# Column-tiled pooling scores for three blocks, loads of a batch spread out, the 2-chunk unit last

## The chip, the cores and the metric

The kernel runs on one core of a Trainium2 chip. A core has five engines that run at the same time and wait for one another through semaphores: TensorE (PE in the profile; its weight loads are shown apart as PEld), VectorE (DVE), ScalarE (ACT), GpSimd (POOL) and SyncE (SP). Data move between main memory and the on-chip memory by DMA; GpSimd and SyncE issue the DMAs here. Matmuls write to PSUM, [...], and DVE or ACT take the results out.

The metric is the device time of one launch in microseconds. The kernel before took 338.13 us (median of 5 runs, 337.91 to 340.12).

## The reference

Two operators follow one another. The first pools a batch's 12,544 tokens into 32 rows by attention from 32 fixed rows (the inducing points), and then lets each token attend to these 32 rows. The second is a feed-forward layer with the larger of two projections.

```python
B, N, m, C = (4, 12544, 32, 128)          # x: (B, N, C), inducing: (m, C)
def mab(q, kv):
    s = scale * (q @ kv.transpose(0, 2, 1))
    a = exp(s - s.max(-1)) ; a /= a.sum(-1) + 1e-09
    return a @ kv
h = mab(I, x)                             # 32 pooled rows per batch
y = mab(x, h)                             # (B * N, C) tokens
out = maximum(y @ w1, y @ w2) @ w_out     # d_ff = 1024
```

The types are float32 in and out.

## The kernel before

The 12,544 tokens of a batch lie as 128 partitions by 98 chunks. A chunk is one column of 128 tokens. Blocks of 16 chunks are called p1 blocks; there are six of them and one of 2 chunks. Inside, x is kept in half precision, once as loaded (`xn`, ten rotating tiles) and once transposed (`xT`, two tiles, one for odd batches and one for even ones).

**Pooling.** For every block, the scores of 128 tokens against the 32 inducing rows are a matmul with the transposed x as weights (`u_scores`, L226, for batch 0; `p1_scores`, L324, for the others). ScalarE takes the exponential into a tile `et` (L235, L333). A matmul with `xn` as weights and `et` as moving data adds up the pooled rows `h` (L260, L346). The sums of the exponentials come from a matmul with a column of ones in batch 0 (L251), and from additions on GpSimd into `eacc` in the other batches (L363, L366). There, `small_fold` (L373) folds the 16 chunks of `eacc` to one in four additions on GpSimd, and `small_h` multiplies it with ones on TensorE (L380) and scales `h`. `small_hwd` (L440) and `small_m1` (L460) then prepare the weights of the second part for that batch.

**Batch 0** comes first and has nothing to hide behind. Its blocks are cut into units; the last blocks are cut finer, and `units` is reordered so that the unit of 2 chunks comes before the last three units (L83). All loads of the units are issued by GpSimd in the order of `units` (L179, L125), the first block by SyncE. The loop at L718 and the lines after it (L726 to L742) write out the order of TensorE's work: transposes of unit i on TensorE (`u_transpose`, L210, copied out by DVE and ACT at L215 and L218), scores of unit i-1, accumulation of unit i-2. After the last unit come the loads of batch 1 (L743), `u_h` with eight more transposes (L271), `u_hwd` (L408), and the first staged blocks.

**The main part** is a sequence of 196 bursts (L803). A burst writes four PSUM banks with the projections of up to 512 columns (L564); DVE (L595) or ACT (L599) take them out with a maximum against zero, and one output tile of an earlier burst is finished with 16 matmuls (L626), a DVE multiplication (L652) and, every second one, a store (L662). The stores of batches 0 to 2 are issued by GpSimd, the others by SyncE. Batch 0 has bursts 0 to 48, batch 1 has 49 to 97, batch 2 has 98 to 146 and batch 3 has 147 to 195.

Between the bursts, `jobs` hold the pooling of the next batch, put there by `at(g, ...)` (L772 to L787). A job runs after the burst with its number, in program order. For the batch after batch b, with `first[b]` the first burst of b: the transposes by DMA (`transpose_batch`, seven DMAs on SyncE, behind a one-element copy on GpSimd at L135 that waits for the last load), the scores and the accumulation of each block, the loads of the batch after that (`load_x`, L120, seven DMAs on GpSimd, one every two bursts, behind the one-element copy of L143), and then the four small steps: fold, h, hwd and m1. For batch 1 they come after bursts 40, 43, 44 and 45, for batches 2 and 3 after 40, 42, 43 and 44 of the batch that runs.

**What sets the order.** Every engine works through its own instructions in program order. The program order is written out by hand as described; which of DVE and ACT takes a bank out, and which bank is used, is decided while the program is built, by a small model of engine times (`Model`). GpSimd's order is that of the calls: stores, loads, additions, folds and the one-element copies stand in one line. Each DMA that GpSimd issues uses one of eight semaphores in turn.

Of the kernel before, what the change touches and what calls it, by code (L numbers as in the profile page):

```python
# [9 lines left out]
F16 = mybir.dt.float16  # L10
F32 = mybir.dt.float32
AF = mybir.ActivationFunctionType
# [39 lines left out]
def kernel(  # L52
# [9 lines left out]
    nc = tc.nc  # L62
    B, N, C = x.shape
    M = inducing.shape[0]
# [4 lines left out]
    scale = 1.0 / math.sqrt(C)  # L69
    HS = 2.0**-14  # L70
    P1B = 16
# [3 lines left out]
    units = []  # L75
    for i, (_, n) in enumerate(p1_blocks):
# [3 lines left out]
            units += [(i, 0, n // 2), (i, n // 2, n // 2)]  # L80
        else:
            units.append((i, 0, n))
    units = units[:-4] + units[-1:] + units[-4:-1]  # L83
    NU = len(units)
    last = NU - 4

    consts = ctx.enter_context(tc.tile_pool(name="consts", bufs=1))
    big = ctx.enter_context(tc.tile_pool(name="big", bufs=1))
    etp = ctx.enter_context(tc.tile_pool(name="etp", bufs=7))
    e2p = ctx.enter_context(tc.tile_pool(name="e2p", bufs=5))  # L90
    smp = ctx.enter_context(tc.tile_pool(name="smp", bufs=2))
    relup = ctx.enter_context(tc.tile_pool(name="relup", bufs=3))
# [7 lines left out]
    model = Model()  # L100
    uid = [0]

    def bank(shape, dtype=F32):
        i = model.bank()
        uid[0] += 1
        return i, psum.tile(shape, dtype, name=f"ps{uid[0]}", tag=f"bank{i}", bufs=1)
# [6 lines left out]
    xT_tiles = [big.tile([128, K, 128], F16, name=f"xT{i}", tag=f"xT{i}") for i in range(2)]  # L113

    def xn_of(b, i):
        return xn_tiles[(NP1 * b + i) % NXN]
# [47 lines left out]
    inducingT = consts.tile([C, M], F16, name="inducingT")  # L164

    with tc.manual_schedule(engines={ET.PE, ET.DVE, ET.Activation, ET.Pool, ET.SP}):
# [28 lines left out]

        st = [dict() for _ in range(B)]


        pool0 = {}

        def u_transpose(i):
            t, g0, n = units[i]
            xn = xn_of(0, t)
            step = 8
            for g in range(g0, g0 + n, step):
                m = min(step, g0 + n - g)
                bi, ps = bank([128, 8, 128], F16)
                end = 0.0
                for j in range(m):
                    nc.tensor.transpose(ps[:, j, :], xn[:, g + j, :], identity16)  # L210
                    end = model.pe(0.056)
                k = p1_blocks[t][0] + g
                dst = xT_tiles[0][:, k : k + m, :]
                if i >= last - 2 or (g // step) % 2 == 0:
                    nc.vector.tensor_copy(out=dst, in_=ps[:, 0:m, :])  # L215
                    model.bank_free[bi] = model.ev("DVE", 64 * m, end)
                else:
                    nc.scalar.copy(out=dst, in_=ps[:, 0:m, :])  # L218
                    model.bank_free[bi] = model.ev("ACT", 128 * m, end)

        def u_scores(i):
            t, g, n = units[i]
            k = p1_blocks[t][0] + g
            bi, ps = bank([128, P1B * M])
            for j in range(n):
                nc.tensor.matmul(  # L226
                    out=ps[:, j * M : (j + 1) * M],
                    lhsT=xT_tiles[0][:, k + j, :],
                    rhs=inducingT,
                    start=True,  # L230
                    stop=True,
                )
                end = model.pe(0.025, model.bank_free[bi])
            et = etp.tile([128, P1B, M], F16, name=f"et_0_{i}", tag="et")
            nc.scalar.activation(  # L235
                out=et[:, 0:n, :], in_=ps[:, 0 : n * M], func=AF.Exp, scale=scale
            )
            model.bank_free[bi] = model.ev("ACT", n * M, end)
            pool0["et", i] = et

        def u_accum(i):
            t, g, n = units[i]
            et = pool0.pop(("et", i))
            xn = xn_of(0, t)
            if i == 0:
                for name in ("h", "sum"):
                    pool0[name] = bank([128, 512])
                    model.bank_free[pool0[name][0]] = 1e9
            for j in range(0, n, 4):
                w = min(4, n - j) * M  # L250
                nc.tensor.matmul(  # L251
                    out=pool0["sum"][1][0:w, 0:1],
                    lhsT=et[:, j : j + w // M, :],
                    rhs=ones16,
                    start=(i == 0 and j == 0),
                    stop=(i == NU - 1 and j + 4 >= n),
                )
                model.pe(0.025)
            for j in range(n):
                nc.tensor.matmul(  # L260
                    out=pool0["h"][1][:, 0:M],
                    lhsT=xn[:, g + j, :],
                    rhs=et[:, j, :],
                    start=(i == 0 and j == 0),
                    stop=(i == NU - 1 and j == n - 1),
                )
                model.pe(0.025)
# [422 lines left out]
        bi, ps = bank([128, 512])  # L690
# [6 lines left out]
        for q in range(4):  # L697
            r = slice(32 * q, 32 * (q + 1))
            nc.vector.tensor_copy(
                out=same_m[r, :, :], in_=identity32[r, None, r].broadcast_to((32, 4, M))  # L700
# [17 lines left out]
        for i in range(last - 1):  # L718
            u_transpose(i)
            if i >= 1:  # L720
                u_scores(i - 1)
            if i >= 2:
                u_accum(i - 2)
            if i < last - 2:
                keep_warm(1)
        u_transpose(last - 1)  # L726
        u_scores(last - 2)
        u_accum(last - 3)
        u_transpose(last)
        u_scores(last - 1)  # L730
        u_transpose(last + 1)
        u_accum(last - 2)
        u_transpose(last + 2)
        u_scores(last)
        u_accum(last - 1)
        u_transpose(last + 3)
        u_scores(last + 1)
        u_scores(last + 2)
        u_accum(last)
        u_scores(last + 3)  # L740
# [14 lines left out]
        for b in range(B):  # L755
            blks = [blk for blk in flat if blk.b == b]
            lead_in = 3 if b == 0 else 0
            for i, blk in enumerate(blks):
                j = i if i < lead_in else i - (i - lead_in) % 2
# [9 lines left out]
        def at(g, f, *a):  # L769
            jobs.setdefault(g, []).append((f, *a))  # L770

        for b in range(B - 1):  # L772
            nb, g = b + 1, first[b]

            t0, l0 = (9, 24) if b == 0 else (-3, 16)
            at(g + t0, transpose_batch, nb)
            if nb + 1 < B:
                at(g + l0, hold_loads, nb)
            for i in range(NP1):
                s = g + (14 + 4 * i if b == 0 else 5 + 5 * i)  # L780
                at(s, p1_scores, nb, i)
                at(s + 2, p1_accum, nb, i)
                if nb + 1 < B:
                    at(g + l0 + 2 * i, load_x, nb + 1, i)
            d = 1 if b == 0 else 0
            for s, f in ((40, small_fold), (42, small_h), (43, small_hwd), (44, small_m1)):
                at(g + s + (0 if f is small_fold else d), f, nb)  # L787


        def load_wf():  # L790
# [64 lines left out]
```

The softmax here doesn't subtract the row's maximum and nothing guards it: scores larger than these inputs give would overflow.

## Time and profile before

| | before |
|---|---|
| time, median of 5 | 338.13 us |
| time of the profiled execution | 338.73 us |
| its span, from the first to the last instruction | 337.0 us |
| TensorE busy | 329.0 us (98%) |
| weight loads busy | 263.1 us (78%) |
| DVE busy | 297.0 us (88%) |
| ScalarE busy | 271.5 us (81%) |
| GpSimd busy | 94.6 us (28%) |
| granted TensorE clock | 0.999 |

The page sums one execution. Its busy times count an engine's own instructions, and its chain follows the end of the program back to what released each step. A line of groups or of the timeline names the source line, the engine, what is written and read with its shape, and at the end the idle time before it with what ended that idle time. In the timeline the first two numbers are the start and the length in us, and xN means that N instructions in a row were merged. The matmuls' ends are modelled, so the starts are the better numbers for them.

### The profile page before, as it was taken

To read this page: it belongs to the slowest core of one execution; us is meant where nothing else is said; L and a number is where in the kernel's file an instruction comes from. 1 tells how busy PE (TensorE), PEld (TensorE's weight loads), DVE (VectorE), ACT (ScalarE), POOL (GpSimd) and SP (SyncE) were. 2 spreads that over 40 slices of the span, in tenths; PEclk is the share of its full clock that TensorE was granted. 3 is DMA by queue.
4 is the path that set the end of the run, shared out by engine and by line. 5 is a ranking of instruction groups with operands and counts; after the bars stand their busy time and mean duration, and the time that the engine had idled before them with its cause. 6 is when DMAs were issued, how large, how long until landed. Compare 5 with 4: busy or idle time off the path is not lost.

```text
span 337.0 us, 14526 instructions
## 1 busy us (share of the span) xinstructions
PE 329.0 (98%) x6352; PEld 263.1 (78%) x6352; DVE 297.0 (88%) x628; ACT 271.5 (81%) x523; POOL 94.6 (28%) x166
## 2 busy tenths in 40 slices
PE   8999999999999999999999999999999999999995
PEld 3776787888878878888877878888777777878875
DVE  1459999999989999999998999999998998999993
ACT  4749978777898887887898877787899989888881
POOL 6242113176741234542341232332252100000000
PEclk9999999999999999999999999999999999999999
DMA  8999899999919986994219992221221222222222
GB/s 213 208 207 215 195 194 196 218 257 234 265 74 227 223 189 161 191 247 136 95 67 189 241 211 79 97 95 64 96 97 65 111 95 75 94 90 95 96 97 109
DMA packets 54143, 51.47 MB, mean 153 GB/s; under 512 B 41536, under 2 KB 42464, under 8 KB 54080
## 3 DMA queue, kind: packets, MB, share of 16 engines
q0 software_dynamic: 11552, 32.38, 38.1%
q1 hardware_dynamic: 42528, 18.17, 25.8%
q8 instruction: 49, 0.80, 1.0%
q14 instruction: 14, 0.11, 0.1%
HBM read 28.33 MB, written 25.69 MB: 160 GB/s over the span
## 4 chain that ended last, share of the span: by engine, by line
PE 91%; DMA 4%; ACT 2%; DVE 1%; POOL 1%; issue 1%; POOLq 0%
PE ps L626 57%; PE ps L564 19%; PE ps L579 4%; DMA xn<-in_x_dram 4%; PE ps L324 2%; PE ps L346 2%; PE ps L499 2%; ACT relu L599 2%; DVE o L652 1%; POOL xn L125 1%; PE ps L520 1%; DVE relu L595 1%; PE ps L210 1%; PE ps L260 0%; PE ps L440 0%
## 5 line engine op out<-in xcount | busy, mean ns | idle before, releaser
L599 ACT ACTIVATE relu<-ps 128x512 f16<-128x512 f32 x445 | 235.9, 601 | 41.6 <-PE ps L564 29.7
L595 DVE TENSOR_SCALAR relu<-ps 128x512 f16<-128x512 f32 x339 | 218.0, 679 | 5.0 <-PE ps L564 3.9
L626 PE MATMUL ps<-woutp,relu 128*128 128x128 f16 x3136 | 208.7, 220 | 0.0
L626 PEld LDWEIGHTS <-relu 128*128 128x128 f16 x3136 | 175.6, 98 | 31.3 <-issue 21.6
L652 DVE TENSOR_TENSOR o<-ps,rp 128x256 f32<-128x256 f32 x196 | 81.7, 417 | 16.3 <-PE ps L626 11.6
L662 POOL DMA_DIRECT2D out_dram<-o x75 | 41.3, 551 | 149.7 <-DVE o L652 102.2
L564 PE MATMUL ps<-e,hwd 32*128 32x256 f16 (+1 forms) x1632 | 82.3, 268 | 0.7 <-ACT relu L599 0.2
L564 PEld LDWEIGHTS <-hwd 32*128 32x128 f16 x1632 | 26.9, 92 | 19.0 <-issue 3.5
L579 PE MATMUL ps<-m,e 32*128 32x128 f16 x372 | 29.8, 214 | 0.8
L579 PEld LDWEIGHTS <-e 32*128 32x128 f16 x372 | 18.3, 92 | 7.1 <-issue 4.2
L366 POOL TENSOR_TENSOR eacc<-eacc,et 128x512 f32<-128x512 f32 (+1 forms) x18 | 18.5, 1030 | 0.3
L333 ACT ACTIVATE et<-ps 128x512 f16<-128x512 f32 (+1 forms) x21 | 11.4, 545 | 5.1 <-PE ps L324 5.1
L120 POOL DMA_DIRECT2D xn<-in_x_dram x21 | 11.4, 545 | 4.4 <-DMA xn<-in_x_dram 1.8
L215 DVE COPY xT<-ps 128x1024 f16<-128x1024 f16 (+2 forms) x10 | 5.8, 596 | 5.9 <-PE ps L210 5.8
L509 ACT ACTIVATE e<-ps 128x512 f16<-128x512 f32 (+1 forms) x21 | 10.9, 578 | 0.0
L324 PE MATMUL ps<-inducingT,xT 128*128 128x32 f16 x294 | 10.6, 176 | 0.3 <-ACT relu L599 0.3
L346 PE MATMUL ps<-et,xn 128*128 128x32 f16 x294 | 10.6, 176 | 0.0
L324 PEld LDWEIGHTS <-xT 128*128 128x128 f16 x294 | 9.5, 96 | 0.4 <-issue 0.4
L346 PEld LDWEIGHTS <-xn 128*128 128x128 f16 x294 | 9.5, 96 | 0.0
L499 PE MATMUL ps<-xT,hT 128*32 128x512 f16 (+2 forms) x120 | 8.7, 350 | 0.0
L191 PE MATMUL ps<-warm 128*128 128x512 f16 x22 | 7.5, 484 | 1.2 <-DVE warm L167 1.2
L210 PE MATMUL ps<-identity,xn 128*128 128x128 f16 x98 | 7.3, 219 | 0.9 <-DMA xn<-in_x_dram 0.5
(79 smaller groups left out, 120.8 us busy)
## 6 DMA issues: line engine op xcount, KB each, us to landing
out_dram<-o POOLq DMA_DIRECT2D x72, 256.0 KB, 3.7
xn<-in_x_dram POOLq DMA_DIRECT2D x21, 512.0 KB, 8.9
out_dram<-o SPq DMA_DIRECT2D x24, 256.0 KB, 2.0
xf<-in_x_dram SPq DMA_DIRECT2D x2, 512.0 KB, 4.1
wf<-in_moe_w_dram SPq DMA_DIRECT2D x2, 512.0 KB, 5.4
xn<-in_x_dram POOLq DMA_DIRECT2D x3, 256.0 KB, 12.2
out_dram<-o POOLq DMA_DIRECT2D x3, 128.0 KB, 5.1
xT<-xn SPq DMA_TRANSPOSE x21, 7.2
```

The costliest lines, as they stand in the source:

```text
L120: nc.gpsimd.dma_start(out=xn_of(b, i)[:, 0:n, :], in_=xr[b, :, k0 : k0 + n, :])
L324: nc.tensor.matmul(out=ps[:, j * M : (j + 1) * M], lhsT=xT_tiles[b % 2][:, k0 + j, :], rhs=inducingT, start=True, stop=True,)
L346: nc.tensor.matmul(out=ps[:, 0:M], lhsT=xn[:, j, :], rhs=et[:, j, :], start=(j == 0), stop=(j == n - 1),)
L366: nc.gpsimd.tensor_add(out=acc, in0=acc, in1=et[:, 0:n, :])
L499: nc.tensor.matmul(out=ps[32 * q : 32 * (q + 1), 0 : self.width], lhsT=st[self.b]["hT4"][:, 32 * q : 32 * (q + 1)], rhs=xT[:, q % self.g], ...
L564: nc.tensor.matmul(out=ps[:, jj * w : (jj + 1) * w], lhsT=st[blk.b]["hwd"][r, 128 * jb : 128 * (jb + 1)], rhs=blk.e2[r, 128 * self.t0 : 12 ...
L579: nc.tensor.matmul(out=part.fin[q][1][:, 128 * s : 128 * (s + 1)], lhsT=part.blk.e2[r, 128 * tt : 128 * (tt + 1)], rhs=st[part.blk.b]["m1" ...
L595: nc.vector.tensor_scalar(out=dst, in0=src, scalar1=0.0, scalar2=None, op0=ALU.max)
L599: nc.scalar.activation(out=dst, in_=src, func=AF.Relu)
L626: nc.tensor.matmul(out=o, lhsT=self.relu[:, jb, q, tt, :], rhs=woutp[:, jb, :], start=(start and s == 0 and jb == 0), stop=(not start and ...
L652: nc.vector.tensor_mul(self.osb[:, h : h + 2, :], ps[:, 0:256].rearrange("p (s c) -> p s c", s=2), rp.broadcast_to((128, 2, 128)),)
L662: eng.dma_start(out=outr[blk.b, :, k : k + nst, :], in_=self.osb[:, 0:nst, :])
```

## The change

Five edits are made together.

- `units` is no longer reordered: the unit of 2 chunks is the last one, in the loads and in TensorE's work. The lines that write out the end of batch 0 get another order (an accumulation or the scores now stand in other places between the transposes).
- For the first three units, all of 16 chunks, the scores are turned round: the inducing rows are the weights and the transposed x moves, four matmuls of 512 columns into the four groups of 32 columns of the array (`col_scores`). The exponential gives `eT`, with the inducing rows on the partitions, and a DVE transpose in blocks of 32 by 32 turns it into `et` (`col_turn`).
- The matmul with the column of ones always takes four chunks; for the unit of 2 chunks DVE clears the two missing chunks of `et` first.
- The loads of the next batch but one are put after every third burst instead of every second.
- The small steps fold, h, hwd and m1 come after bursts 41, 43, 44 and 45 for every batch. For batch 1 this moves the fold by one burst, for batches 2 and 3 all four.

TensorE's program has 72 instructions fewer, DVE's has six more.

```diff
--- before.py
+++ after.py
@@ -80,13 +80,13 @@
             units += [(i, 0, n // 2), (i, n // 2, n // 2)]
         else:
             units.append((i, 0, n))
-    units = units[:-4] + units[-1:] + units[-4:-1]
     NU = len(units)
     last = NU - 4
 
     consts = ctx.enter_context(tc.tile_pool(name="consts", bufs=1))
     big = ctx.enter_context(tc.tile_pool(name="big", bufs=1))
     etp = ctx.enter_context(tc.tile_pool(name="etp", bufs=7))
+    eTp = ctx.enter_context(tc.tile_pool(name="eTp", bufs=3))
     e2p = ctx.enter_context(tc.tile_pool(name="e2p", bufs=5))
     smp = ctx.enter_context(tc.tile_pool(name="smp", bufs=2))
     relup = ctx.enter_context(tc.tile_pool(name="relup", bufs=3))
@@ -194,6 +194,35 @@
 
 
         st = [dict() for _ in range(B)]
+
+        def col_scores(b, k0, n, name):
+
+
+            bi, ps = bank([128, P1B * M])
+            for q in range(4):
+                r = slice(32 * q, 32 * (q + 1))
+                nc.tensor.matmul(
+                    out=ps[r, 0 : n * 32],
+                    lhsT=inducingT,
+                    rhs=xT_tiles[b % 2][:, k0 : k0 + n, r],
+                    start=True,
+                    stop=True,
+                    tile_position=(0, 32 * q),
+                )
+            end = model.pe(32 * n / 2400, model.bank_free[bi], "col")
+            eT = eTp.tile([128, P1B * M], F16, name=f"eT_{name}", tag="eT")
+            nc.scalar.activation(
+                out=eT[:, 0 : n * M], in_=ps[:, 0 : n * M], func=AF.Exp, scale=scale
+            )
+            model.bank_free[bi] = model.ev("ACT", n * M, end)
+            return eT, model.bank_free[bi]
+
+        def col_turn(eT, ready, n, name):
+            et = etp.tile([128, P1B, M], F16, name=f"et_{name}", tag="et")
+            nc.vector.transpose(
+                et[:, 0:n, :].rearrange("p k m -> p (k m)"), eT[:, 0 : n * M]
+            )
+            return et, model.ev("DVE", n * M, ready)
 
 
         pool0 = {}
@@ -221,6 +250,9 @@
         def u_scores(i):
             t, g, n = units[i]
             k = p1_blocks[t][0] + g
+            if i < 3:
+                pool0["et", i], _ = col_turn(*col_scores(0, k, n, f"0_{i}"), n, f"0_{i}")
+                return
             bi, ps = bank([128, P1B * M])
             for j in range(n):
                 nc.tensor.matmul(
@@ -232,6 +264,8 @@
                 )
                 end = model.pe(0.025, model.bank_free[bi])
             et = etp.tile([128, P1B, M], F16, name=f"et_0_{i}", tag="et")
+            if n % 4:
+                nc.vector.memset(et[:, n : n + 4 - n % 4, :], 0.0)
             nc.scalar.activation(
                 out=et[:, 0:n, :], in_=ps[:, 0 : n * M], func=AF.Exp, scale=scale
             )
@@ -247,10 +281,9 @@
                     pool0[name] = bank([128, 512])
                     model.bank_free[pool0[name][0]] = 1e9
             for j in range(0, n, 4):
-                w = min(4, n - j) * M
                 nc.tensor.matmul(
-                    out=pool0["sum"][1][0:w, 0:1],
-                    lhsT=et[:, j : j + w // M, :],
+                    out=pool0["sum"][1][:, 0:1],
+                    lhsT=et[:, j : j + 4, :],
                     rhs=ones16,
                     start=(i == 0 and j == 0),
                     stop=(i == NU - 1 and j + 4 >= n),
@@ -728,13 +761,13 @@
         u_accum(last - 3)
         u_transpose(last)
         u_scores(last - 1)
+        u_accum(last - 2)
         u_transpose(last + 1)
-        u_accum(last - 2)
+        u_scores(last)
         u_transpose(last + 2)
-        u_scores(last)
         u_accum(last - 1)
+        u_scores(last + 1)
         u_transpose(last + 3)
-        u_scores(last + 1)
         u_scores(last + 2)
         u_accum(last)
         u_scores(last + 3)
@@ -781,10 +814,9 @@
                 at(s, p1_scores, nb, i)
                 at(s + 2, p1_accum, nb, i)
                 if nb + 1 < B:
-                    at(g + l0 + 2 * i, load_x, nb + 1, i)
-            d = 1 if b == 0 else 0
-            for s, f in ((40, small_fold), (42, small_h), (43, small_hwd), (44, small_m1)):
-                at(g + s + (0 if f is small_fold else d), f, nb)
+                    at(g + l0 + 3 * i, load_x, nb + 1, i)
+            for s, f in ((41, small_fold), (43, small_h), (44, small_hwd), (45, small_m1)):
+                at(g + s, f, nb)
 
 
         def load_wf():
```

## The prediction

> **What bounds the kernel now.** I read the page first (busy times, chain, costliest groups), then the timeline stage by stage, and last the trace's semaphore times for landings.
>
> ```profile
> PE 329.0 (98%) x6352; PEld 263.1 (78%) x6352; DVE 297.0 (88%) x628; ACT 271.5 (81%) x523; POOL 94.6 (28%) x166
> ...
> q8 instruction: 49, 0.80, 1.0%
> ...
> PE 91%; DMA 4%; ACT 2%; DVE 1%; POOL 1%; issue 1%; POOLq 0%
> ...
> L626 PE MATMUL ps<-woutp,relu 128*128 128x128 f16 x3136 | 208.7, 220 | 0.0
> ```
>
> TensorE is 91% of the chain that ended last, and its output matmuls have no idle time before them. From 36 us to 320 us I find one stall of TensorE over 0.3 us, at 46.3 us. There a microsecond added to TensorE's path is a microsecond of time, and one saved on another engine is worth nothing. The stage before it is different:
>
> ```profile
> 15.87 0.69 DVE L215 COPY xT<-ps 128x1024 f16<-128x1024 f16 x1 [1.32 <-PE ps L210]
> ...
> 16.89 0.77 PE L210 MATMUL ps<-identity,xn 128*128 128x128 f16 x8 [0.16 <-DMA xn<-in_x_dram]
> ...
> 20.55 0.87 ACT L235 ACTIVATE et<-ps 128x256 f16<-128x256 f32 x3 [0.51 <-PE ps L226]
> ...
> 23.17 0.10 PEld L271 LDWEIGHTS <-w1h 128*128 128x128 f16 x1 [0.88 <-issue]
> ...
> 25.21 0.40 PE L564 MATMUL ps<-e,hwd 32*128 32x128 f16 x16
> ```
>
> To 16.89 us TensorE waits for loads of x. From there a chain of transposes, scores, exponentials and sums ends at 21.6 us. Then comes a hole of 0.88 us that no semaphore ends, at 23.17. Counted along TensorE's stream, the late weight load is record 705; record 449, exactly 256 earlier, also starts about 0.13 us late (17.25). The page has 49 packets of 16 KB on the instruction queue for 12,704 matrix instructions, one per 259. So I read the hole as an instruction block that came late[...].
>
> The one later stall, and what feeds it:
>
> ```profile
> 38.76 0.54 POOL L662 DMA_DIRECT2D out_dram<-o  x1 [4.68 <-DVE o L652]
> 39.30 0.18 POOL L135 COPY xT<-xn 1x1 f16<-1x1 f16 x1
> ...
> 39.50 10.90 SPq L129 DMA_TRANSPOSE xT<-xn  x3
> ...
> 46.33 0.48 PEld L324 LDWEIGHTS <-xT 128*128 128x128 f16 x16 [0.40 <-issue]
> ```
>
> The scores of batch 1 wait here for the first transposed tile, which landed at 46.23. Its gate on GpSimd (L135) stood behind a store, and behind the last load of batch 1, which landed at 38.67.
>
> The fold of the row sums, batch 2, and the matmul that reads it (L380):
>
> ```profile
> 166.69 0.56 POOL L662 DMA_DIRECT2D out_dram<-o  x1 [2.13 <-DVE o L652]
> ...
> 167.27 2.00 POOL L373 TENSOR_TENSOR eacc<-eacc 128x256 f32<-128x256 f32 x4
> ...
> 169.53 0.56 POOL L662 DMA_DIRECT2D out_dram<-o  x1 [0.26 <-DVE o L652]
> 169.90 0.36 PE L380 MATMUL ps<-eacc,ones 128*128 128x32 f32 x2
> ...
> 170.19 0.40 PE L564 MATMUL ps<-e,hwd 32*128 32x256 f16 x8
> ```
>
> The fold ends at 169.27, 0.58 us before L380's weight load wants it (169.85). The fold starts when the store before it has gone, not when its data are ready. The next store goes at 169.53.
>
> [...] L499 issues 8 column-tiled matmuls of 512 columns in 0.54 us, 0.27 us for four.
>
> **The change part by part.**
>
> *Column-tiled scores, three blocks.* Each removes 16 matmuls and adds four: about 0.40 us of issue becomes 0.27. Bounds: 0.13 us saved each, or 4 x 0.21 = 0.85 if nothing overlapped, 0.45 lost each. Cover: blocks 0 and 1 lie before the wait for x at 13.2 us, block 2 before that at 16.89, and its exponential starts only when ScalarE's copy of block 3 ends (15.3). I take 0.
>
> *Three DVE transposes.* Block 2 has the latest: exponential done at 15.82[...] Cost 0[...].
>
> *The 2-chunk unit last, a memset of about 0.06 us, sums always 128 wide.* I replayed the tail with the same durations. The last copy and exponential are shorter, but two 8-chunk units now follow one another; the last accumulation issues at 21.58 either way. I take 0, bounds -0.3 to +0.3. The load only changes places in one queue.
>
> *72 instructions fewer on TensorE.* 3 x 12 matmuls with their weight loads. The block border that fell on record 705 now falls 72 records further, in the middle of burst 0. [...] Without the hole, w1T ends 0.85 us earlier, hwd's last eviction is at 24.2 instead of 25.08 (its w2h landed at 21.95 and woutp at 23.56, so the loads allow it), and burst 0 starts at about 24.33: 0.88 us earlier[...]. Bounds: 0 if the block is late again, 0.95.
>
> *What becomes of it.* At the scores of batch 1 the gain meets its cap. The store goes at 37.9 and the gate could run at 38.4, but the last load still lands at 38.67, because the loads fill the DMA engines and their bytes are the same. GpSimd's lag after a landing lies between 0.1 us and the 0.5 us seen at L143 (landed 67.57, copy 68.05), so the gate runs at 38.75 to 39.15 instead of 39.30, and tile 0 comes 0.15 to 0.55 us earlier. TensorE simply waits longer. Kept: **-0.35 us**, bounds +0.2 to -0.6.
>
> *Loads every three bursts instead of two.* In batch 0 the last load moves behind the fold and a store, from 85.45 to about 94.0; before, small loads took 5 to 8 us. So it should be there by 100.6, where L135 takes it. Earlier loads move past stores and adds with no one waiting: POOL is 28% busy, the stores have 4 output buffers. 0; were it late, the transposes would still have several us until the scores at 110.8.
>
> *Small steps one burst later.* For batch 1 only the fold's place changes, and in program order nothing stands between it and the accumulation before it: no move, 0. For batches 2 and 3 all four steps move one burst. In GpSimd's order one more store now stands before the fold, the one at 169.53. It waits for the DVE product of 168.82 to 169.23, goes at 169.53, takes 0.56; then the fold, 170.11 to 172.11. L380's weight load without the move was at 169.85; one burst later, without L380's own 0.29 us in between, it is wanted at 169.85 + 1.24 = 171.09. It gets its data at about 172.17: a stall of 1.08 us. Queued behind it on TensorE is everything: the next burst, and through it ScalarE and DVE. For batch 3 the same: store 247.47, fold 248.05 to 250.05, wanted at 249.02, stall 1.10. **+2.18 us**, bounds 1.7 (DVE product a little earlier) to 2.5. The later steps (hwd, m1, m1d) have two bursts of room and cost 0.
>
> Sum: -0.35 + 2.18 = **+1.83 us**. The profiled execution took 338.73 (span 337.0 and 1.7 around it) and would take 340.6; it lies 0.6 above the median of 338.13, which becomes **339.96**.
>
> **The rivals.**
> A (the sum above), 339.7 to 340.5. For it: the 0.58 us of slack against a shift of 2.84 us in the fold's start and 1.24 us in L380's. Against it: spans on GpSimd are rough.
> B: the prologue gives nothing back, since the instruction block is late again or the DVE transpose takes over 1.1 us. Then +2.2 to +2.9: 340.3 to 341.0. [...]
> C, the other side: the gain of the prologue passes L324, since the last load of batch 1 lands before the store has gone at 38.4. Its price is up to the whole 0.88 us; from 0.49 us kept the sum stays under 0.5%. Then 339.3 to 339.8, not measurably slower. For it: a lag of 0.1 us on GpSimd alone would keep 0.55. Against it: the bytes ahead of that load are unchanged.
> D: the move does not put the fold late, the store before it going sooner. It would have to go at 168.45 for no stall; TensorE finishes the matmuls for its product at 168.63, so at most half of it can go. 337.5 to 338.8. That the loads are spread without any reader noticing is part of A.
>
> **How the numbers follow.** A 0.50, B 0.20, C 0.20, D 0.07, other 0.03. About 0.5% (1.7 us) is what a measurement of this kernel can tell. A lies a little above that border (339.82), so of its 0.50 I put 0.35 slower and 0.15 same; B is slower, C and D same, the rest faster. Slower 0.55, same 0.42, faster 0.03. The range from 338.6 to 341.0 leaves out most of D and scatter at both ends; A's own range is 339.7 to 340.5.
>
> **What would show it.** Right: in the changed kernel a wait of about 1.1 us before L380 twice, ended by the fold on GpSimd, and none the first time; no hole without a releaser near 22 us; burst 0 near 24.3; the scores of batch 1 waiting about 1 us for their transposed tile. Wrong: a fold that begins before the second store, a hole inside burst 0, or a DVE transpose near 1 us.

## The result and the profile after

The changed kernel takes 340.24 us (median of 44 runs, 339.54 to 343.8). The kernel before, run beside it, takes 339.36 us (79 runs). The ratio is 1.0044, 95% interval 1.0031 to 1.0057: 1.5 us slower, a little inside the 0.5% border, which the interval crosses. The two medians lie only 0.88 us apart and the means 1.37. The profiled executions agree with the ratio: 340.25 against 338.73 us, spans of 338.5 and 337.0.

In 58 of the 137 executions of the kernel before that were run beside the experiments the mean TensorE clock is 0.993 to 0.995 and the median time 339.62 us, in the others the clock is 0.998 or more and the median 338.32, so that its median can move by over a microsecond with the mix, while the changed kernel had a clock under 0.997 in only 2 of 44 (the section on the hardware comes back to this).

The page of the changed kernel, same lines as before:

```profile
PE 329.1 (97%) x6316; PEld 262.1 (77%) x6316; DVE 300.4 (89%) x634; ACT 270.8 (80%) x521; POOL 94.8 (28%) x166
...
q8 instruction: 49, 0.80, 0.9%
...
PE 85%; DMA 5%; DVE 4%; POOL 2%; ACT 2%; issue 1%; POOLq 0%
...
L659 PE MATMUL ps<-woutp,relu 128*128 128x128 f16 x3136 | 208.7, 220 | 0.0
```

TensorE's work is unchanged: 329 us, and the output matmuls (now L659) cost 208.7 us as before. The span grew by 1.5 us in which TensorE did not work. GpSimd has gone from 1% to 2% of the chain. The page alone says no more than that.

The timeline of the prologue:

```profile
15.81 0.71 DVE L222 STREAM_TRANSPOSE et<-eT 128x512 f16<-128x512 f16 x1 [1.23 <-ACT eT L214]
16.44 0.65 DVE L244 COPY xT<-ps 128x1024 f16<-128x1024 f16 x1
16.57 0.16 PEld L284 LDWEIGHTS <-et 128*128 128x128 f16 x4 [0.46 <-DVE et L222]
...
22.19 0.32 PEld L304 LDWEIGHTS <-w1h 128*128 128x128 f16 x4
...
24.49 0.40 PE L597 MATMUL ps<-e,hwd 32*128 32x128 f16 x16
```

The hole of 0.88 us inside the transposes of w1 (now L304) is gone, and burst 0 starts at 24.49 instead of 25.21, 0.72 us earlier. The DVE transpose, which no row of before showed, takes 0.71 us, and TensorE waits 0.46 us for the third one.

The gate of the first transposed tile, and the scores that wait for it:

```profile
38.04 0.54 POOL L695 DMA_DIRECT2D out_dram<-o  x1 [4.68 <-DVE o L685]
38.58 0.18 POOL L135 COPY xT<-xn 1x1 f16<-1x1 f16 x1
...
38.78 9.98 SPq L129 DMA_TRANSPOSE xT<-xn  x3
...
45.66 0.48 PEld L357 LDWEIGHTS <-xT 128*128 128x128 f16 x16 [0.45 <-issue]
```

In both traces the gate ran directly behind the store, here at 38.58 instead of 39.30. The last load of batch 1, which landed at 38.41 (before 38.67), did not hold it. The tile landed at 45.55 (before 46.23), and the scores start at 45.66 (before 46.33): 0.67 us of the prologue's gain passed.

The fold of batches 2 and 3, and the row-sum matmul that reads it (L406 and L413 now):

```profile
169.27 0.54 POOL L695 DMA_DIRECT2D out_dram<-o  x1 [2.29 <-DVE o L685]
169.83 2.00 POOL L406 TENSOR_TENSOR eacc<-eacc 128x256 f32<-128x256 f32 x4
...
171.88 0.30 PEld L413 LDWEIGHTS ps<-eacc,ones 128*128 128x128 f32 x2 [0.94 <-POOL eacc L406]
...
248.65 2.00 POOL L406 TENSOR_TENSOR eacc<-eacc 128x256 f32<-128x256 f32 x4
250.71 0.30 PEld L413 LDWEIGHTS ps<-eacc,ones 128*128 128x128 f32 x2 [0.93 <-POOL eacc L406]
```

Two new stalls of 0.94 and 0.93 us, both ended by the fold, which stands behind one more store. The row sums of batch 1, at 92.8 us, have none.

When the starts of the output matmuls of the two traces are laid over one another, the changed kernel's are 0.72 us earlier after the prologue, lose 0.45 at 122.9 us, 0.88 at the first of these stalls and 0.90 at the second, and end 1.51 us later, which is the difference of the spans. The loss at 122.9 us was not in the forecast:

```profile
122.86 0.10 PEld L532 LDWEIGHTS <-hT 128*32 128x32 f16 x4 [0.53 <-issue]
```

Again a wait that no semaphore ends. Counted along TensorE's stream of weight loads, matmuls and its few waits, it is record 4545, which is 193 + 17 x 256, and the packet on the instruction queue that is counted to it, in order, had ended at 121.58, 1.28 us earlier. So it is read here as the same thing as the hole at 23.17 us in the kernel before, at another place.

### The profile page after: what moved, and what is told of

Its sections match the earlier page's. It is cut to its first block, busy times and chain, and to the rows that moved or that the text cites. A ratio compares the mean times of both kernels' runs of the same rounds, so it can differ in the third digit from the quotient of the medians.

```text
span 338.5 us, 14460 instructions
## 1 busy us (share of the span) xinstructions
PE 329.1 (97%) x6316; PEld 262.1 (77%) x6316; DVE 300.4 (89%) x634; ACT 270.8 (80%) x521; POOL 94.8 (28%) x166
## 4 chain that ended last, share of the span: by engine, by line
PE 85%; DMA 5%; DVE 4%; POOL 2%; ACT 2%; issue 1%; POOLq 0%
PE ps L659 53%; PE ps L597 18%; PE ps L612 4%; DMA xn<-in_x_dram 3%; PE ps L357 2%; PE ps L532 2%; PE ps L379 2%; DMA xT<-xn 2%; DVE relu L628 2%; DVE o L685 1%; ACT relu L632 1%; POOL eacc L406 1%; PE ps L239 1%; PE ps L553 0%; POOL out_dram L695 0%
## 5 line engine op out<-in xcount | busy, mean ns | idle before, releaser
L659 PE MATMUL ps<-woutp,relu 128*128 128x128 f16 x3136 | 208.7, 220 | 0.0
L659 PEld LDWEIGHTS <-relu 128*128 128x128 f16 x3136 | 175.7, 98 | 31.1 <-issue 21.4
```

What stands on the lines that cost most here:

```text
L659: nc.tensor.matmul(out=o, lhsT=self.relu[:, jb, q, tt, :], rhs=woutp[:, jb, :], start=(start and s == 0 and jb == 0), stop=(not start and ...
```

## The experiments

The theory, F: the time is lost because the fold has one more store ahead of it on GpSimd, while the row sums come only 1.24 us later; the prologue gives a little back because 72 fewer records move an instruction block. The rivals: the other moved steps cost the time, or the spread loads or the unit order do, or the prologue gives nothing. Ratios are to the kernel before, run beside each. The spans of two single profiles compare only roughly: the first transposes of x start between 7.57 and 8.62 us after the first instruction, in kernels with the old and the new prologue alike (7.61 and 7.58 in the two profiles above).

**1. The four small steps put back, all else of the change kept.**

```diff
-            for s, f in ((41, small_fold), (43, small_h), (44, small_hwd), (45, small_m1)):
-                at(g + s, f, nb)
+            d = 1 if b == 0 else 0
+            for s, f in ((40, small_fold), (42, small_h), (43, small_hwd), (44, small_m1)):
+                at(g + s + (0 if f is small_fold else d), f, nb)
```

> The changed kernel with the small steps of the kernel before (fold at 40; h, hwd, m1 at 43, 44, 45 for batch 1 and 42, 43, 44 for the others). Theory F (the two stalls come from the fold that now stands behind one more store): no wait before the matmul of the row sums, the two losses of about 0.9 us each are gone, so 1.8 us less than the changed kernel: about 0.3 us faster than before (ratio 0.998 to 1.000), span near 336.7. Rival L (the loads spread out or the prologue cost the time, the wait at the fold only takes up idle time that would appear elsewhere): the span stays within 0.5 us of 338.5.

338.52 us, ratio 0.9995 (0.9975 to 1.0015). Its timeline at the fold of batch 2:

```profile
167.46 2.00 POOL L406 TENSOR_TENSOR eacc<-eacc 128x256 f32<-128x256 f32 x4
169.72 0.56 POOL L695 DMA_DIRECT2D out_dram<-o  x1 [0.27 <-DVE o L685]
170.03 0.30 PEld L413 LDWEIGHTS ps<-eacc,ones 128*128 128x128 f32 x2
```

The fold is ahead of the store again, it ends 0.57 us before it is wanted, and no wait stands behind the weight load. The median is 1.72 us under that of the changed kernel; the two stalls cost 0.88 + 0.90 = 1.78. The steps carry all of the loss.

**2. The kernel before with the small steps moved, nothing else.**

```diff
-            d = 1 if b == 0 else 0
-            for s, f in ((40, small_fold), (42, small_h), (43, small_hwd), (44, small_m1)):
-                at(g + s + (0 if f is small_fold else d), f, nb)
+            for s, f in ((41, small_fold), (43, small_h), (44, small_hwd), (45, small_m1)):
+                at(g + s, f, nb)
```

> The kernel before with only the small steps moved as in the change. Theory F: two waits of 0.9 to 1.1 us before the matmul of the row sums in batches 1 and 2, none in batch 0, and 1.8 to 2.2 us more than before: ratio 1.005 to 1.0065. Rival L: under 0.5 us more, ratio under 1.0015.

340.96 us (6 runs), ratio 1.006 (1.0037 to 1.0083): about 2 us slower than before. What the trace answers on the row-sum matmul (L380 in this kernel), idle time before it and how often:

```profile
  POOL eacc L373: 3.3, 4
```

That is two stalls, each counted once for the weight load (0.92 and 0.92) and once for the matmul behind it. The cause is there without any other part of the change.

**3. The kernel before with the spread loads alone** (`l0 + 3 * i` for `l0 + 2 * i`).

> The kernel before with only the loads put after every third burst. My sum put this at 0: ratio 0.999 to 1.001, no new wait on TensorE. Rival S (the spread loads are what made an instruction block late at 122.9 us in the changed kernel, by moving transfers into the time of the transposes by DMA): about 0.45 us more, with a hole of 0.4 us without a releaser on TensorE between 115 and 130 us.

339.15 us, ratio 1.0001 (0.9984 to 1.0017). Nothing, as forecast. The rival falls too: no instruction block is late between 115 and 130 us (one is at 97.87, by 0.94 us). This profile happened to catch a half-clock stretch, which is used below.

**4. The kernel before with the prologue's edits alone** (column tiles, DVE transposes, sums 128 wide, units and their order).

> The changed kernel with the small steps and the spacing of the loads of the kernel before, so only the new order of batch 0, the column-tiled scores and the DVE transposes are left. Theory: burst 0 starts 0.7 us earlier than before (24.5 instead of 25.2), the scores of batch 1 keep 0.4 to 0.7 of it, and the time is 0.4 to 0.7 us less than before: ratio 0.998 to 0.999. Rival: it gives nothing that lasts, ratio 0.9995 to 1.001.

338.83 us, ratio 1.0003 (0.9983 to 1.0023). From the first transpose to burst 0 its trace has 16.80 us where before has 17.60, so the prologue is shorter by 0.8. The ratio shows none of it: the median is 0.41 us under that of the 43 executions of the kernel before beside it, but 0.5 over those of them at full clock (338.31). In the profile, 0.96 and 0.86 us stand at 142.1 and 148.8 us without a releaser, at block borders. The clock was full in all 14 executions.

**5. The steps put back, and 72 records added to TensorE's warm-up** (41 small matmuls for 5 large ones, on a spare bank), so that the block borders fall where they did. No work is left out; dummy matmuls are added.

> The steps-back version with 72 more records on TensorE ahead of the first transposes: 13 warm-up matmuls of 512 columns instead of 18, and 41 of 32 columns (the output is unchanged). All work after it is the same; only the border of the instruction blocks goes back to the eighth transpose of w1h. Theory I (the gain of the prologue is the instruction block that no longer comes late there): the hole of 0.4 to 0.9 us without a releaser is back at record 705 near 23 us, burst 0 starts 0.5 to 0.9 us later after the first transposes than in the steps-back version, the execution loses the half-clock stretch again in some of its runs, and the median is 0.4 to 0.8 us above the steps-back version. Rival W (the gain is TensorE's shorter work and the new order): no hole, and the median of the steps-back version within 0.2 us.

339.14 us, ratio 0.9999 (0.9981 to 1.0016). It came out 0.6 over experiment 1, but not by the way the test was made for: the hole at the transposes of w1 is only 0.12 us, and another wait stands ahead of it.

```profile
14.62 1.07 PE L239 MATMUL ps<-identity,xn 128*128 128x128 f16 x16 [1.24 <-DMA xn<-in_x_dram]
```

In this profile an instruction packet ran from 12.54 to 13.49 us, in the time of a load of x. That load landed at 14.58, while in the other twelve traces it landed between 13.10 and 13.37. So this run doesn't isolate the block; whether the packet held the load up, one profile doesn't show.

**6. The steps put back, and the three blocks scored as before** (no column tiles and no DVE transposes; unit order, 128-wide sums and spread loads of the change kept).

```diff
-            if i < 3:
+            if i < 0:
                 pool0["et", i], _ = col_turn(*col_scores(0, k, n, f"0_{i}"), n, f"0_{i}")
```

> The steps-back version with the scores of all units as before the change (no column tiles, no DVE transposes; 72 records more on TensorE). Theory I: as with the added records, the hole is back at record 705, the half clock in some of its runs, median 0.4 to 0.8 us above the steps-back version. Rival W: the column-tiled scores save time themselves and their loss costs 0.1 to 0.4 us without any hole; or the DVE transposes cost time and the version is 0.1 to 0.3 us faster.

339.29 us, ratio 1.0008 (0.999 to 1.0026); 0.77 over experiment 1.

```profile
23.16 0.10 PEld L304 LDWEIGHTS <-w1h 128*128 128x128 f16 x1 [0.83 <-issue]
```

The hole is back, at record 705, as in the kernel before. The transposes of w1 begin at 21.59 us, no later than in the changed kernel (21.72), so the column tiles did not bring the work ahead of them forward. The gain of the new prologue fits the 72 records that they save, and not faster scores; since experiment 5 failed to do so, no run moves the block alone. And the clock was under 0.997 in 11 of 22 executions.

**7. The steps and the unit order put back** (`units` reordered again, the tail written out as before; column tiles and DVE transposes kept).

> The steps-back version with the order of units of the kernel before: the 2-chunk unit ahead of the last three, in loads and in TensorE's work. My sum put the order of units at 0, with bounds of 0.3 us both ways: median within 0.3 us of the steps-back version, and the accumulations end within 0.15 us of 21.65. Rival U (the earlier landing of the last load of batch 1, 38.41 instead of 38.67, came from the unit order): that load lands 0.2 to 0.3 us later again, measured from the landing of the first load.

338.32 us, ratio 0.9995 (0.9977 to 1.0013). The order of the units is worth nothing that can be measured. The rival of the expectation falls as well: the last load of batch 1 lands 33.92 us after the first load, against 33.98 in the changed kernel.

**8. The steps put back, and the first scores of batch 1 one burst later** (`max(15, 14 + 4 * i)` for `14 + 4 * i`).

> The steps-back version with the first scores of batch 1 one burst later (15 instead of 14). Theory: the wait of 0.4 to 0.5 us for the first transposed tile goes away, since the burst in between takes 1.4 us, so 0.3 to 0.5 us less than the steps-back version where that wait occurs; no other wait appears, since the accumulation keeps two bursts. Rival: the wait moves to the second tile or to the store queue and the median stays within 0.1 us.

338.54 us, ratio 0.9984 (0.9963 to 1.0005). The scores now start at 47.02 us with no wait, so the cap at the first tile is gone, and the span of its profile is 336.8. The median is that of experiment 1, whose own profile had no wait for that tile either: it stands in 5 of the 13 profiles only. In this profile 0.43 us without a releaser stands at 77.2 us.

**9. The changed kernel with the fold alone one burst earlier** (`(40, small_fold)`); the other three steps stay where the change put them.

> The changed kernel with the fold of batches 1 and 2 one burst earlier (offset 40 for 41), nothing else: on GpSimd it stands again ahead of the store that runs before it in the changed kernel. The row sums and the three small steps after it stay a burst early. Theory F (the store and the lag ahead of the fold make it late, and nothing else of the earlier steps costs): no wait of TensorE on GpSimd at the row-sum matmul (L413), the two stalls of 0.93 us gone, median that of the run with the steps put back, 338.5 us, 1.7 us under the changed kernel, ratio to the kernel before 0.997 to 1.002. Rival (it is the earlier small steps themselves, not the fold's place behind the store): 340.2 us, ratio 1.003 to 1.006.

339.05 us (22 runs), ratio 1.001 (0.9991 to 1.0029).

```profile
167.40 1.99 POOL L406 TENSOR_TENSOR eacc<-eacc 128x256 f32<-128x256 f32 x4
169.67 0.56 POOL L695 DMA_DIRECT2D out_dram<-o  x1 [0.27 <-DVE o L685]
171.31 0.30 PEld L413 LDWEIGHTS ps<-eacc,ones 128*128 128x128 f32 x2
```

The fold now has 1.9 us to spare, there is no wait at L413, and the span is 1.51 us under the changed kernel's, although its first transposes start 0.53 us later. The median fell by 1.2 and not by the 1.7 expected; the other five kernels with the new prologue and no stall have medians of 338.32 to 338.88. The rival, that the other three steps cost the time, falls.

**10. The changed kernel with the fold of every batch at burst 43**: a larger dose of the same cause.

> The changed kernel with the fold of every batch at offset 43 for 41, the row sums still at their place: a dose test. In batches 1 and 2 one more store now stands ahead of the fold on GpSimd, in batch 0 a store and the small load. Theory F: in batches 1 and 2 the fold runs at about 172.7 to 174.7 us and its like 79 us later, the row sums want it at about 170.95, so the stalls grow from 0.93 to about 3.8 us each, and batch 0 gets one of about 3 us where it had none; in all 8.5 to 9 us over the changed kernel, about 349 us, ratio 1.025 to 1.032, with all of the added time in front of L413 under GpSimd's name. Rival (the two stalls seen are incidental, and a later fold is taken up by slack elsewhere, such as the bursts behind it running closer together): under 345 us.

353.92 us (4 runs), ratio 1.0438 (1.0397 to 1.0478), 13.7 us over the changed kernel. The profiled execution is the fastest of the four, at 352.19, and its clock the highest (0.985, the others 0.976 to 0.981); its span is 350.4, 11.9 us over the changed kernel's. The rival falls; the size was missed. The timeline at batch 2, and what the trace answers on L413:

```profile
174.71 0.54 POOL L695 DMA_DIRECT2D out_dram<-o  x1 [2.29 <-DVE o L685]
175.26 1.99 POOL L406 TENSOR_TENSOR eacc<-eacc 128x256 f32<-128x256 f32 x4
...
177.31 0.64 PE L413 MATMUL ps<-eacc,ones 128*128 128x32 f32 x2 [3.58 <-POOL eacc L406]
```

```profile
  POOL eacc L406: 20.3, 6
```

The three stalls, at the weight loads, are 2.89, 3.75 and 3.75 us, in all 10.40. Without the 1.87 that the changed kernel already had, that is 8.5 us, the lower end of the expectation. The other 3.4 us stand behind the two long stalls, in the table of windows (stretch, its length, busy time of PE, PEld, DVE, ACT and POOL, then the granted clock):

```profile
177.00:181.00 4.00, 3.69 (x32) 2.78 (x32) 1.78 (x5) 1.57 (x3) 0.25 (x1) 0.50 0.00 0
181.00:185.00 4.00, 4.00 (x56) 2.33 (x56) 3.39 (x6) 3.11 (x8) 0.69 (x2) 0.76 0.01 4
...
261.00:265.00 4.00, 3.79 (x36) 2.63 (x40) 2.06 (x5) 1.57 (x3) 0.15 (x1) 0.57 0.01 2
```

After the stall TensorE is working, at half its clock. This had been left out of the expectation.

**11. A version meant to beat both**: experiment 7 with the later first scores of experiment 8.

> A version meant to beat both: the changed prologue (column tiles, three VectorE transposes, spread loads), the unit order and the small steps of the kernel before, and the first scores of batch 1 one burst later, so that they do not wait for their tile. Parts measured before: steps back takes 1.7 us off the changed kernel, unit order 0, first scores 0 in the median though the wait in the profile was gone. If these add: 338.2 to 338.5 us, ratio to the kernel before 0.996 to 0.999, so at most just outside no change. If the wait taken from the first tile comes back at a late instruction block or elsewhere: 338.5 to 338.9 us.

338.88 us (14 runs), ratio 1.0001 (0.9983 to 1.0019). It beats the changed kernel and is level with the kernel before. Of all versions, experiment 8 has the lowest ratio, and its interval still holds 1.

## Why the prediction was right, step by step

The forecast was 339.96 us, +1.83. The measured ratio stands for +1.5 us, and the median of 340.24 lies in A's own range. Whether the kernel is slower by more than 0.5%, on which the forecast put 0.55, the interval leaves open. A's main step is shown by the runs; two of its terms were mis-sized, and one loss was left out.

That the number came so close is in part luck, twice. Four of the five executions behind the base of 338.13 us lie under 338.7, with those of the kernel before at full clock, and the changed kernel runs at full clock too; from the later median of 339.36 the same sum gives 341.19, outside the stated range. And the two mis-sized terms together made the sum 0.77 us too high, of which a late block that nobody forecast made up 0.45.

- **The fold behind one more store, +2.18.** Right in place, cause and number of stalls (experiments 1, 2, 9 and 10), a fifth too large: 0.94 and 0.93 us, net 0.88 and 0.90, not 1.08 and 1.10. The forecast kept the time of a burst at 1.24 us when it moved L380 by one burst; without the row sums between, the burst after an output tile starts 1.00 us after that tile's matmuls instead of 0.90, so L413 is wanted 0.1 us later.
- **Batch 1's fold: no move, 0.** Right: no wait at 92.8 us.
- **Loads, unit order, 128-wide sums, later hwd and m1: 0.** Right: experiments 3, 7 and 9. The last load of batch 2 went at 93.32 us and landed at 97.42, before the 100.6 by which the forecast needed it.
- **The instruction block moves 72 records, burst 0 earlier by 0.88.** The hole of 0.88 us went with the 72 records and came back at record 705, 0.83 us long, in experiment 6; the gain was 0.72. That the moved block would be there in time was the author's estimate, and so was the length of a DVE transpose, which no row of before showed. It took 0.71 us, and the transposes of w1 began at 21.72 and not 21.61.
- **The cap at the first tile, kept 0.35.** This step failed. "The last load still lands at 38.67" did not hold: it landed at 38.41, ahead of the gate, and 0.67 us passed. That is rival C's mechanism, beyond its point of 0.49. But no effect of the change on the landing is seen: over the 13 profiles it lies between 38.41 and 38.93, in the three with the old prologue between 38.54 and 38.88. The forecast took the one time that it had seen for a fixed one. The lag was mis-sized as well: where the gate did wait for the load (experiments 4 and 8), it ran 0.05 us after the landing, not 0.1 (an estimate) to 0.5 (seen at L143), which at a landing of 38.67 would have kept 0.58. The step didn't decide the result, since the profiled execution then lost 0.45 us to the block at 122.9. By offsets the sum is -0.72 + 0.45 + 0.88 + 0.90 = +1.51.
- **What the medians keep of the prologue.** Less than the profiles. The six kernels with the changed column tiles and no fold stall (experiments 1, 4, 7, 8, 9 and 11) have a median of 338.76 over 100 executions; the kernel before, beside them, 338.99 over 137. That is -0.2 us. Against the executions of the kernel before at full clock (338.32) it is +0.4. So what is left of the gain in the median goes with the half clock, which the changed prologue almost never shows, and which the prediction didn't have. Why executions at full clock don't keep the 0.7 us is open. Late blocks at new places, as in experiments 4, 7 and 8, are one candidate: counted from the first transposes the six profiles take 328.30 to 329.94 us (before 329.35), and the two longest are experiments 4 and 7. But the old prologue is followed by such blocks too (0.71 us in experiment 2, 0.94 in experiment 3). Another candidate is that at full clock the block of the kernel before happened to come earlier; the two profiles that could show it, before and experiment 2, ran at full clock with holes of 0.88 and 0.64 us, which speaks against it. No run here settles it.
- **The other rivals.** B's reason did not hold in the profile (no late block in the prologue, 0.71 us for the DVE transpose), though its number, +2.2, lies only 0.3 above the difference at full clock (340.21 - 338.32 = +1.89), to which A's +1.83 is nearer still. D is excluded by the two stalls.

## What to carry to other kernels

A small step that is moved "one burst later" moves past what stands between on every queue that it uses: ask what its first instruction now stands behind, and whether its reader moved by as much. When an edit changes the number of instructions on TensorE, look at where the waits with no releaser fall before and after: here they stood a multiple of 256 records apart (705 and 4545), and the one of 0.88 us is more than the scores of the three blocks were to save (0.13 us each at most). And a wait of TensorE can cost more than its length: in experiment 10 the clock was at half behind two of them, and the span grew by 3.4 us more than the stalls did. A landing time or a start that one trace shows is one draw: before taking it for a cap, see how far it scatters.

## What the runs showed of the hardware

**Instruction blocks.** The instruction queue moved 49 packets of 16 KB (0.80 MB) in the profile of either kernel, for 12,704 and 12,632 matrix instructions. Records 193 + 256 k of TensorE's stream are called borders here, since the waits without a releaser stand there: 0.88 us at record 705 (23.17 us) in the kernel before, 0.53 us at record 4545 (122.86 us) in the changed one. If the packets are counted to the borders in order, the packets of these two ended at 21.90 and 121.58, 1.27 and 1.28 us before. They had started 3.67 and 4.20 us after the record at the border ahead. Over all borders of the two profiles this ranges from 0.28 us ahead of that record to 4.20 behind it; the median is 1.7 us (kernel before) and 2.5 us (changed) for the borders from 57 to 125 us, and 0.2 and 0.1 after 215. In the kernel before the DMA share of the profile is 0.75 to 1.21 from 50 to 125 us and 0.19 to 0.28 after 215, so the late packets go with loads and DMA transposes; no run tests that these are the cause. Neighbouring borders were 5.4 to 8.4 us apart in the kernel before. That TensorE waits there for its instructions is the author's reading: the traces show the place, the length and the packets, not what the wait is for. Other profiles had such waits at other borders, up to 0.96 us long, so that two single profiles can differ by 1 us and more for this alone (0.96 and 0.86 in experiment 4).

**The half clock.** The profile of experiment 3 caught it in the prologue:

```profile
7.10:24.20 17.10, 15.70 (x346) 13.50 (x345) 8.09 (x25) 8.46 (x16) 6.20 (x11) 1.00 1.17 208
24.20:27.60 3.40, 3.40 (x40) 2.07 (x38) 1.84 (x5) 1.73 (x5) 0.00 (x0) 0.50 1.07 216
```

TensorE's matmuls have a hole of 0.98 us up to 23.56, with no releaser; from 24.2 to 27.6 us, 3.4 us, the clock is at half (0.50), and then full again. Such a stretch costs up to 1.7 us by estimate, half of its length, which is what a mean clock of 0.995 lacks over 338 us; the two groups of times of the kernel before lie 339.62 - 338.32 = 1.30 us apart. The kernels with the hole had it often (the kernel before in 58 of 137 executions; 2 of 6, 10 of 22 and 11 of 22 in experiments 2, 3 and 6), those without it almost never (2 of 100 in experiments 1, 4, 7, 8, 9 and 11 together; 1 of 14 in experiment 5, with a hole of 0.12 us). The stretch of experiment 6, from 23.9 to 27.3 us, is 3.4 us long too. In experiment 10 the clock is at half for 6.8 us from 176.1 us on, inside one stall of 3.75 us, and for 3.4 us from 261.4, just behind the other, while the stall of 2.89 us at 93 us left it full (1.00 from 92 to 100 us). TensorE needn't be idle all the time ahead of such a stretch: it was busy for 2.42 of the 3.40 us ahead of that of experiment 3 and for 2.63 in experiment 6. Nor does the busy share decide it: a stretch with 0.77 us busy of 3.40 (experiment 10, from 92.3) left the clock full, and so did that of the hole in the profile of the kernel before (from 20.5), with 2.69. Stalls of 0.93 us inside the dense output matmuls did not bring it (2 of 44). What the criterion is, these runs don't tell; the prologue's part in it is a correlation over kernels with and without the hole. Why one execution of a kernel has the stretch and another has not, no run tests.

**Smaller prices.** A 32 by 32 block transpose of 128x512 f16 on DVE took 0.71 us, a fold of four additions on GpSimd 2.00, and the issue of a store 0.54 to 0.60.
